# Attention of two inputs on one core: unread products counted per slot, VectorE's exponentials paced apart and eight a unit, the last units normalised piecewise

## The chip, the core and the metric

One core of a Trainium2 chip. The metric is the device time of one execution in microseconds (us); the median of several runs is quoted, and the spread. Five engines run side by side: TensorE (PE in the profile, its weight loads PEld), VectorE (DVE), ScalarE (ACT), GpSimd (POOL) and SyncE (SP), which issues most transfers.

## The reference

Two attention blocks with 32 heads of 16 columns, on 2048 tokens of 512 columns each, bf16. Block A attends to everything, block B to the last 256 positions. Cut to what matters:

```python
qkv = (x @ wqkv).reshape(B, S, 3, H, Dh)          # S=2048, H=32, Dh=16
scores = einsum("bhqd,bhkd->bhqk", q, k) * Dh ** -0.5
# B alone: positions outside 0 <= i - j < 256 get -1e9
o = einsum("bhqk,bhkd->bhqd", softmax(scores), v).reshape(B, S, D) @ wo
return concatenate([a, b], axis=-1)
```

## The kernel before

Block A alone has 2048 x 2048 x 32 exponentials. Work is cut into *units* (four heads by 512 queries), units into *tiles* (128 keys by 512 queries of one head), and three tiles make a *slot*: three score products on TensorE into a score buffer of three PSUM banks (two such buffers), one exponential of 1536 columns on ScalarE. The values of earlier slots are multiplied into one accumulator bank. Everything else shares one spare bank ("ms"): projections, guard rows, and tiles whose exponential VectorE computes by a bit trick (a copy for each tile, and three passes for each two). The order is fixed in advance by a small pacing model: `PITCH` is a slot, `queued` tells it what VectorE has to do, `by` asks whether that will be done in time.

Some words that come back: a *window slot* is a slot of block B. *Padded keys* are those of the first two groups of heads, projected straight into the layout that the scores need. A *guard row* is an extra row of the queries, made from their absolute values and the largest keys, that takes a bound off the scores before the exponential. An *unread product* is a matmul whose result nobody uses. In the lines of the traces `sps` are the score buffers, `ms` is the spare bank, `op` the accumulator, `pT` what ScalarE's exponentials write, `dy` VectorE's copies of scores and `pD` its own exponentials.

```python
PACE_D = (2, 2, 2, 1)      # groups of four tiles a unit for VectorE, from the ninth unit on
...
def scores(self, slot):    # for the slot after next
    ...
    if b == 0 and self.filled < 2 and jb.inst == 0:
        self.work += 0.22   # a product that nobody reads, to keep TensorE's clock up
        self.nc.tensor.matmul(sps[:, 0, 0:WARM], lhsT=kT[...], rhs=qT[...], start=True, stop=True)
    ... # the real scores then overwrite it
...
def slots(self):
    ...
    groups[-1:-1] = poly    # values of VectorE's tiles: all ahead of the unit's last group
...
def q_evac(...):            # projection of queries; guard() two slots later
        gs = self.tile([8, 512], BF16, "gs", 1)          # one buffer
        self.nc.vector.tensor_copy(out=gs[:], in_=b[0:8, :])
        self.nc.sync.dma_start(qd[:, DH, :], gs[:])
...
def end(self, i, p, g):     # the last two units of block A
    rec = self.tile([P, 512], FP32, "oc", 2)
    nc.vector.reciprocal(out=rec[:], in_=op[:])           # straight from the accumulator
    ... copy op to osb, then for both halves: ones x rec on TensorE, multiply on VectorE
...
def run(self):
    for s, sl in enumerate(slots):
        self.exps(sl); ...; self.scores(slots[s + 2]); self.values(); ...
        # one list of tasks, VectorE's tiles among them (they count double)
        credit = min(credit + min(rate, 2.5), 3.0)
        ...
        while credit >= 1.0 and self.fill(s, tasks, done):
            credit -= 1.0; self.filled += 1; self.work += 0.4
        if self.work < 0.8 and self.open is None and self.by(self.freed, 0.9):
            self.busy(2 if self.work < 0.6 else 1)        # unread products into the spare bank
```

Of the kernel before, what the change touches and what calls it, by code (L numbers as in the profile page):

```python
# [14 lines left out]
P = 128  # L15
H = 32
DH = 16
# [25 lines left out]
PACE_D = (2, 2, 2, 1)  # L43
XRING = 5
FIRST_B = 6
WARM = 512
# [56 lines left out]

class _Kernel:

    def __init__(self, ctx, tc, tensors, out):
        self.tc, self.nc = tc, tc.nc
        self.t = tensors
        self.out = out
        pool = lambda name, **kw: ctx.enter_context(tc.tile_pool(name=name, **kw))  # L110
        self.consts = pool("consts", bufs=1)
        self.sb = pool("sb", bufs=1)
        self.ps = pool("ps", bufs=1, space=bass.MemoryType.PSUM)
        self.dram = pool("dram", bufs=1, space=bass.MemoryType.DRAM)
        self.xT, self.w, self.wo, self.kT, self.v, self.qT = {}, {}, {}, {}, {}, {}
        self.acol, self.negas, self.oT = {}, {}, {}
        self.op, self.od = {}, {}
        self.later = []
        self.slot = self.ended = self.closed = -1
        self.pend, self.guards, self.dq = [], [], []  # L120
        self.open = self.mid = None
        self.filled = 2
        self.vec = self.freed = self.op_free = 0.0
        self.last_poly = -1
# [17 lines left out]
    def busy(self, n):  # L142

        b = self.bank()
        for _ in range(n):
            self.nc.tensor.matmul(b[:], lhsT=self.ident[:], rhs=self.junk, start=True,  # L146
                                  stop=True)
# [35 lines left out]
    def more_constants(self):  # L183
# [26 lines left out]
        top = self.tile([8, 512], BF16, "gs", 1)  # L210
        nc.gpsimd.memset(top[:], TOP)
        for t in self.qd:
            nc.gpsimd.dma_start(t[:, DH + 1, :], top[:])
# [145 lines left out]
    def q_evac(self, i, p, pr, bank, copy):  # L359
        qs = self.tile([P, 512], BF16, "qs", 2)  # L360
        mq = self.tile([P, 512], BF16, "mq", 2)
# [9 lines left out]
        def guard():  # L371
            b = self.bank()
            self.nc.tensor.matmul(b[0:8, :], lhsT=w[:], rhs=mq[:], start=True, stop=True)
            gs = self.tile([8, 512], BF16, "gs", 1)
            self.queued(OP, True)
            self.nc.vector.tensor_copy(out=gs[:], in_=b[0:8, :])  # L376
            self.nc.sync.dma_start(qd[:, DH, :], gs[:])
# [36 lines left out]
    def last_out(self, i, p):  # L414
# [12 lines left out]

        def first():
            for qc in range(4):
                for c in range(NC):  # L430
                    mm(qc, c)

        def finish():
            obs = self.tile([P, SLOT, 512], BF16, "pT", 6)
            for qc in range(4):
                mm(qc, NC)
                ob = obs[:, qc, :] if qc < SLOT else self.tile([P, D], BF16, "ob", 2)[:]
                (nc.scalar.copy if qc % 2 else nc.vector.tensor_copy)(out=ob, in_=banks[qc])
                q0 = p * 512 + qc * P
                (nc.scalar if qc % 2 else nc.sync).dma_start(  # L440
                    self.out[q0:q0 + P, i * D:(i + 1) * D], ob)
# [12 lines left out]
    def pad_k_evac(self, gg, c, bank):  # L454
# [4 lines left out]
        else:  # L459
# [3 lines left out]
                                     op=ALU.max, apply_absolute_value=True)  # L463

    def pad_q_evac(self, gg, bank):
        nc = self.nc
        if gg == 0:
# [3 lines left out]
        mq = self.tile([P, 512], BF16, "mq", 2)  # L471
        nc.vector.tensor_scalar(out=mq[:].bitcast(U16), in0=qT.bitcast(U16),
                                scalar1=0x7FFF, scalar2=None, op0=ALU.bitwise_and)
        return mq

    def pad_guard(self, gg, mq):
# [8 lines left out]
        qT = self.padq[:, gg, :]  # L485
        nc.vector.scalar_tensor_tensor(out=qT, in0=qT, scalar=self.top[:], in1=b[:],
# [29 lines left out]
    def scores(self, slot):  # L516
        sps = self.ps.tile([P, SLOT, 512], FP32, name="sps", tag="sps", bufs=2)
        for b, jb in enumerate(slot["jobs"]):
# [4 lines left out]
            if b == 0 and self.filled < 2 and jb.inst == 0:  # L523

                self.work += 0.22
                kT, k0 = self.kT[jb.inst, jb.g // 2, jb.subs[0][0] // 4]
                self.nc.tensor.matmul(sps[:, 0, 0:WARM], lhsT=kT[:, gg, k0:k0 + P],  # L527
                                      rhs=qT[:, gg, 0:WARM], start=True, stop=True)
# [40 lines left out]
    def poly_steps(self, group):  # L569
# [3 lines left out]
        p, g, kt = group[0].p, group[0].g, group[0].subs[0][0]  # L573

        def step(jb):
# [3 lines left out]
            if half == 0:  # L579
# [4 lines left out]
            kT, k0 = self.kT[0, g // 2, kt // 4]  # L584
            k0 += (kt % 4) * P
            nc.tensor.matmul(b[:], lhsT=kT[r, g % 2, k0:k0 + P],  # L586
                             rhs=self.qT[0, p, g // 2][r, g % 2, :], start=True, stop=True,
                             tile_position=(32 * jb.j, 0))
# [29 lines left out]
    def values(self):  # L618


        while self.pend:
            group, last = self.pend[0]
            if any(jb.ready is None or jb.ready > self.slot for jb in group):
                return
            key = group[0].key
# [5 lines left out]
            op = self.op[key]  # L631
            self.pend.pop(0)
            self.work += 0.33
            for jb in group:
                h = 4 * jb.g + jb.j
                for kt, q0, q1, o in jb.subs:
                    self.nc.tensor.matmul(op[32 * jb.j:32 * jb.j + 32, q0:q1],  # L637
                                          lhsT=self.v[jb.inst, kt][:, h * VP:h * VP + 32],
                                          rhs=jb.pT[:, o:o + q1 - q0],
                                          start=(jb.j not in self.started), stop=False,  # L640
                                          tile_position=(0, 32 * jb.j), skip_group_check=True)
                    self.started.add(jb.j)
            if last:
                self.epilogue(*key)
                self.ended = self.slot

    def load_ends(self):

        self.wend = self.tile([P, 2, D], BF16, "kTb", KRING_B)
# [7 lines left out]
    def end(self, i, p, g):  # L657


        nc = self.nc  # L660
        op = self.op[i, p, g]
        ones = self.tile([P, 32], FP32, "den", 2)
        nc.gpsimd.memset(ones[:], 1.0)
        rec = self.tile([P, 512], FP32, "oc", 2)
        nc.vector.reciprocal(out=rec[:], in_=op[:])
        osb = self.tile([P, 512], FP32, "osb", 2)
        (nc.scalar.copy if self.mid else nc.vector.tensor_copy)(out=osb[:], in_=op[:])
        if self.mid:
            self.mid()
        o = self.tile([P, 512], BF16, "oTa", 5)  # L670
        b = self.bank()
        for q in (slice(0, 256), slice(256, 512)):
            for j in range(GH):
                r = slice(32 * j, 32 * j + 1)
                nc.tensor.matmul(b[32 * j:32 * j + 32, q], lhsT=ones[r, :], rhs=rec[r, q],
                                 start=True, stop=True, tile_position=(32 * j, 32 * j))
            nc.vector.tensor_mul(out=o[:, q], in0=osb[:, q], in1=b[:, q])
        self.closed = self.slot
        self.queued(5.0, True)
        self.op_free = self.vec  # L680
        self.oT.setdefault((i, p), []).append(o)

    def epilogue(self, i, p, g):
# [4 lines left out]
        if (i, p) == (0, NPASS - 1) and g >= NG - 2:  # L688
            self.end(i, p, g)
# [40 lines left out]
    def start(self):  # L730
# [71 lines left out]
        nv = 4  # L802
        for t in range(nv):
            vb = tile_("op", 1) if t % 2 else self.bank()
            self.v_mm(0, t, vb[:], range(NC), (0, HV))
            self.v_evac(0, t, vb[:], nc.scalar.copy, (0, HV))
        self.busy(3)
        self.pad_guard(0, mq)
        self.busy(4)
# [3 lines left out]
    def slots(self):  # L813
# [9 lines left out]
        for u in order:  # L823
            groups = [u[k:k + GH] for k in range(0, len(u), GH)]
            k = ua.index(u) if u[0].inst == 0 else -1
            n = PACE_D[k % len(PACE_D)] if k >= FIRST_D else 0
            poly, groups = groups[:n], groups[n:]
# [4 lines left out]
            groups[-1:-1] = poly  # L832
            pend += [(group, group is groups[-1]) for group in groups]
# [71 lines left out]

    def fill(self, s, tasks, done):
# [8 lines left out]
        t = self.cur  # L915
        t["steps"].pop(0)()
# [5 lines left out]
    def run(self):  # L922
        done = set(self.start())
        self.vec = self.freed = self.op_free = 0.0
        slots, self.pend = self.slots()
        tasks = self.plan(slots, done)
        credit = 0.0
        self.scores(slots[0])
        self.scores(slots[1])
        for s, sl in enumerate(slots):  # L930
# [8 lines left out]
            self.work = 0.33  # L939
# [9 lines left out]
            rate, total = 0.0, 0  # L949
            for t in tasks:  # L950
                if t["nb"] <= s:
                    total += len(t["steps"]) * (2 if t["name"][0] == "d" else 1)
                    rate = max(rate, total / max(1, t["due"] - s))
            credit = min(credit + min(rate, 2.5), 3.0)
            self.filled = 0
# [4 lines left out]
            while credit >= 1.0 and self.fill(s, tasks, done):  # L960
                credit -= 1.0
                self.filled += 1
                self.work += 0.4
            if self.work < 0.8 and self.open is None and self.by(self.freed, 0.9):
                self.closed = s
                self.busy(2 if self.work < 0.6 else 1)
        while self.pend:
            self.slot += 1
            self.values()
        assert not tasks and not self.guards, [t["name"] for t in tasks]  # L970
# [52 lines left out]
```

## Time and profile before

| | |
|---|---|
| time, median of 4 runs | 1098.9 us (1088.8 to 1101.4) |
| busy: ScalarE / TensorE / VectorE | 94% / 89% / 58% |
| mean clock of TensorE in the profiled run | 0.970 |
| exponentials on ScalarE | 771, 727 of them of 1536 columns |

The prediction below shows the lines that carry the reading. Two more stretches matter. The first is TensorE's timeline just before one of the half-clock stretches (start, length, engine, line, operation, result and operands, shape, count, and in brackets the idle time before it):

```profile
820.13 0.38 PE L527 MATMUL sps<-qTa,kTa 128*128 128x512 bf16 x1 [0.63 <-ACT pT L559]
820.44 0.39 PE L532 MATMUL sps<-qTa,kTa 32*128 32x512 bf16 x3
820.76 0.40 PE L637 MATMUL op<-pT,va 128*32 128x512 bf16 x4
821.48 0.38 PE L527 MATMUL sps<-qTa,kTa 128*128 128x512 bf16 x1 [0.31 <-ACT pT L559]
821.79 0.39 PE L532 MATMUL sps<-qTa,kTa 32*128 32x512 bf16 x3
822.11 0.40 PE L637 MATMUL op<-pT,va 128*32 128x512 bf16 x4
822.82 0.59 PE L527 MATMUL sps<-qTa,kTa 128*128 128x512 bf16 x1 [0.31 <-ACT pT L559]
```

These are thin slots: one unread product, three scores, four values, and then idle time. The last line is the same product as the first, but takes 0.59 us instead of 0.38: the clock has been halved in between, although TensorE stood still for no longer than 0.63 us at a time. It stayed halved for 20.5 us.

The second is the start. The guard of the first keys could be subtracted at 20.29, and the first exponential came 2.2 us later:

```profile
20.29 0.75 DVE L486 SCALAR_TENSOR_TENSOR qTa<-qTa,top,ms 128x512 bf16<-128x512 bf16 x1 [1.80 <-PE ms L484]
...
21.09 1.02 PE L146 MATMUL ms<-ident 128*128 128x512 bf16 x4 [0.84 <-DVE qTa L486]
...
22.05 0.60 PE L532 MATMUL sps<-qTa,kTa 32*128 32x512 bf16 x6
22.48 2.79 ACT L559 ACTIVATE pT<-sps 128x1536 bf16<-128x1536 f32 x2 [2.99 <-PE sps L532]
```

Four unread products wait for the spare bank and stand ahead of the first scores.

### The profile page before, as it was taken

The page shows a single profiled execution, that of the slowest core. Times are in us where ns is not written, and L with a number is a line of the kernel's source. Part 1 is how long each engine was busy: PE and PEld are TensorE (multiplying, and loading weights), DVE is VectorE, ACT ScalarE, POOL GpSimd, SP SyncE. Part 2 cuts the span into 40 slices and gives each one's busy share as a digit, 9 for nine tenths or more (in the row PEclk, how much of TensorE's full clock was granted, in tenths as well). Part 3 has the DMA queues.
Part 4 walks back from the last instruction along what each step waited for, and adds up shares of the span by engine and source line. Part 5 has one row for each costly group of instructions (what it writes and reads, how often), then busy time and mean ns, then how long its engine had stood idle before and what let it go on. Part 6 is the DMA issues. An engine that isn't in the chain of part 4 may idle for free.

```text
span 1097.5 us, 18628 instructions
## 1 busy us (share of the span) xinstructions
PE 973.1 (89%) x7583; PEld 322.0 (29%) x7661; DVE 636.7 (58%) x844; ACT 1031.8 (94%) x788; POOL 20.3 (2%) x101
## 2 busy tenths in 40 slices
PE   7899888889988899988998889998899999989877
PEld 4333222233323233222332233323232332322212
DVE  3342231126868578883687755777574776576733
ACT  5899999999999999999999899999998999999976
POOL 6000000000000000000000000000000000000000
PEclk9999999999999999999999899999996999997989
DMA  7021531222412123121130411212101221010101
GB/s 231 1 83 35 135 112 35 63 66 74 117 59 76 44 84 94 59 85 41 51 112 20 123 41 42 81 60 89 45 30 59 76 74 60 31 50 20 58 3 39
DMA packets 72358, 73.04 MB, mean 67 GB/s; under 512 B 22584, under 2 KB 55888, under 8 KB 72272
## 3 DMA queue, kind: packets, MB, share of 16 engines
q1 hardware_dynamic: 69072, 67.88, 20.4%
q10 hardware_dynamic: 2432, 1.84, 0.5%
q0 software_dynamic: 768, 2.13, 0.5%
q8 instruction: 60, 0.98, 0.4%
q14 instruction: 26, 0.21, 0.1%
HBM read 38.65 MB, written 31.07 MB: 64 GB/s over the span
## 4 chain that ended last, share of the span: by engine, by line
ACT 50%; PE 29%; issue 11%; DVE 8%; DMA 1%; SPq 0%; ACTq 0%; DVEq 0%
ACT pT L559 50%; PE sps L532 6%; PE op L637 6%; PE ms L242 6%; PE sps L527 4%; PE sps L541 4%; DVE dy L589 2%; PE ms L586 2%; PE ms L146 1%; DMA kTa<-in_A_x_dram 1%; DVE dh L600 1%; DVE pD L610 1%; DVE gs L376 0%; DVE qs L362 0%; DVE ob L407 0%
## 5 line engine op out<-in xcount | busy, mean ns | idle before, releaser
L559 ACT ACTIVATE pT<-sps 128x1536 bf16<-128x1536 f32 (+2 forms) x771 | 1020.8, 1484 | 46.0 <-PE sps L532 29.7
L527 PE MATMUL sps<-qTa,kTa 128*128 128x512 bf16 x580 | 227.4, 392 | 70.6 <-ACT pT L559 62.6
L532 PE MATMUL sps<-qTa,kTa 32*128 32x512 bf16 x1880 | 259.7, 397 | 1.5 <-ACT pT L559 1.3
L637 PE MATMUL op<-pT,va 128*32 128x512 bf16 x1880 | 193.4, 402 | 0.3 <-DVE osb L695 0.2
L589 DVE COPY dy<-ms 128x512 f32<-128x512 f32 x168 | 115.4, 687 | 132.8 <-PE ms L586 131.3
L532 PEld LDWEIGHTS <-kTa 32*128 32x128 bf16 x1880 | 62.9, 91 | 289.5 <-issue 289.1
L600 DVE SCALAR_TENSOR_TENSOR dh<-dy 128x1024 f32<-128x1024 uint16 x84 | 102.4, 1219 | 1.6
L610 DVE SCALAR_TENSOR_TENSOR pD<-dh,dy 128x1024 uint16<-128x1024 f32 x84 | 102.2, 1217 | 1.1
L604 DVE SCALAR_TENSOR_TENSOR dh<-dy,dh 128x1024 f32<-128x1024 uint16 x84 | 102.0, 1215 | 0.9
L527 PEld LDWEIGHTS <-kTa 128*128 128x128 bf16 x580 | 56.4, 97 | 130.3 <-issue 108.2
L637 PEld LDWEIGHTS <-va 128*32 128x32 bf16 x2048 | 51.2, 94 | 111.2 <-issue 108.6
L541 PE MATMUL sps<-mask,ident 128*128 128x128 bf16 (+1 forms) x640 | 78.7, 249 | 0.0
L586 PE MATMUL ms<-qTa,kTa 32*128 32x512 bf16 x168 | 65.5, 390 | 5.8 <-DVE kst L260 1.2
L695 DVE COPY osb<-op 128x512 f32<-128x512 f32 x62 | 42.7, 689 | 35.1 <-PE op L637 34.9
L532 PE MATMUL sps<-qTb,kTb 32*128 32x384 bf16 (+2 forms) x704 | 59.8, 276 | 3.4 <-ACT pT L559 1.7
L146 PE MATMUL ms<-ident 128*128 128x512 bf16 x172 | 53.7, 382 | 9.7 <-DVE dy L589 2.2
L260 DVE CAST kst<-ms 128x512 bf16<-128x512 f32 x28 | 19.3, 690 | 60.2 <-PE ms L242 60.2
L541 PEld LDWEIGHTS <-ident 128*128 128x128 bf16 x640 | 43.7, 98 | 32.7 <-issue 30.0
L362 DVE TENSOR_SCALAR qs<-ms 128x512 bf16<-128x512 f32 x31 | 21.2, 685 | 48.2 <-PE ms L242 48.0
L407 DVE CAST ob<-ms 128x512 bf16<-128x512 f32 x28 | 19.3, 690 | 47.0 <-PE ms L242 46.8
L242 PE MATMUL ms<-wv,xT 128*128 128x368 bf16 (+2 forms) x171 | 37.4, 315 | 2.9 <-DVE padmax L462 0.8
L637 PE MATMUL op<-pT,vb 128*32 128x384 bf16 (+2 forms) x704 | 38.0, 281 | 0.1
(102 smaller groups left out, 445.1 us busy)
## 6 DMA issues: line engine op xcount, KB each, us to landing
od<-osb SPq DMA_DIRECT2D x62, 256.0 KB
oc<-od SPq DMA_DIRECT2D x31, 256.0 KB
rb<-rd SPq DMA_DIRECT2D x31, 256.0 KB
kTb<-kd SPq DMA_DIRECT2D x16, 256.0 KB
qTb<-qd SPq DMA_DIRECT2D x16, 256.0 KB
qd<-qs SPq DMA_DIRECT2D x31, 128.0 KB
qTa<-qd SPq DMA_DIRECT2D x15, 256.0 KB
kd<-kst SPq DMA_DIRECT2D x28, 128.0 KB
```

The source lines that it names most:

```text
L146: self.nc.tensor.matmul(b[:], lhsT=self.ident[:], rhs=self.junk, start=True, stop=True)
L242: self.nc.tensor.matmul(bank, lhsT=lhs(c), rhs=rhs(c), start=(c == 0), stop=(c == NC - 1))
L527: self.nc.tensor.matmul(sps[:, 0, 0:WARM], lhsT=kT[:, gg, k0:k0 + P], rhs=qT[:, gg, 0:WARM], start=True, stop=True)
L532: self.nc.tensor.matmul(sps[:, b, o:o + q1 - q0], lhsT=kT[r, gg, k0:k0 + P], rhs=qT[r, gg, q0:q1], start=(o == jb.subs[0][3]), stop=not jb ...
L541: self.nc.tensor.matmul(sps[:, b, o:o + P * len(kind)], lhsT=self.ident[:], rhs=m, start=False, stop=True, skip_group_check=True)
L559: nc.scalar.activation(out=pT[:, b:e, :n], in_=sps[:, b:e, :n], func=ACT.Exp, scale=LN2 / 128, bias=-127 * LN2)
L586: nc.tensor.matmul(b[:], lhsT=kT[r, g % 2, k0:k0 + P], rhs=self.qT[0, p, g // 2][r, g % 2, :], start=True, stop=True, tile_position=(32 * ...
L589: nc.vector.tensor_copy(out=y[:, half, :], in_=b[:])
L600: nc.vector.scalar_tensor_tensor(out=st["h"][:], in0=low, scalar=-65536.0, in1=low, op0=ALU.add, op1=ALU.mult)
L604: nc.vector.scalar_tensor_tensor(out=st["h"][:], in0=low, scalar=65536.0 * POLY[1], in1=st["h"][:], op0=ALU.add, op1=ALU.mult)
L610: nc.vector.scalar_tensor_tensor(out=out.bitcast(U16), in0=st["h"][:], scalar=POLY[0] * 2.0 ** -41, in1=flat, op0=ALU.mult, op1=ALU.add)
L637: self.nc.tensor.matmul(op[32 * jb.j:32 * jb.j + 32, q0:q1], lhsT=self.v[jb.inst, kt][:, h * VP:h * VP + 32], rhs=jb.pT[:, o:o + q1 - q0], ...
```

## The change

Its intent: hold TensorE's clock with as few unread products as will do, keep them out of the slots that have no room, give VectorE its tiles in its own rhythm and one seventh more of them, and shorten the start and the end. The core of the diff (cuts marked):

```diff
-PACE_D = (2, 2, 2, 1)
+PACE_D = 2
...
     def scores(self, slot):
-            if b == 0 and self.filled < 2 and jb.inst == 0:
-                self.work += 0.22
-                ... one product of keys and queries
+            if b == 0 and jb.inst == 0:
+                self.busy(sps[:, 0, :], 2 - self.whole)
...
     def q_evac(...)                       # mq becomes a ring of three
-            gs = self.tile([8, 512], BF16, "gs", 1)
-            self.nc.vector.tensor_copy(out=gs[:], in_=b[0:8, :])
+            self.nc.vector.tensor_copy(out=mq[0:8, :], in_=b[0:8, :])
...
     def pad_k_evac(...)
+        self.queued(2 * OP + 0.05, True)
...
     def values(self):
+            late = self.poly_pend.get(key, [])
+            if key in self.op and late and self.done_by(late[0]):
+                self.value(key, late.pop(0))      # VectorE's tiles as they come
+                continue
...
     def end(...)
+        nc.vector.tensor_copy(out=osb[:, q0:q1], in_=op[:, q0:q1])
+        def invert(q):
+            nc.vector.reciprocal(out=rec[:, q:q + 128], in_=osb[:, q:q + 128])
+            ...                                  # the spread comes a slot later
+        self.dq += [lambda q=q: invert(q) for q in range(q0, q1, 128)]
...
     def slots(self):
+            if u is ua[-1]:
+                (groups, ends), n = _parts(groups), 1   # last unit: queries 0-255, then 256-511
...
     def fill(...)
+        self.whole += 1 if t["name"][0] in "dv" else 2
...
     def run(self):
+        polys = [t for t in tasks if t["name"][0] == "d"]
+        tasks = [t for t in tasks if t["name"][0] != "d"]
...
+            if poly_credit >= 1.0 and self.open is None and self.fill(s, polys, done):
+                poly_credit -= 1.0
+            must = self.open is not None
+            while (credit >= 1.0 or must) and self.fill(s, tasks, done):
                 credit -= 1.0
-            if self.work < 0.8 and self.open is None and self.by(self.freed, 0.9):
-                self.closed = s
-                self.busy(2 if self.work < 0.6 else 1)
+                must = False
...
     # start(): the first value projections go to score banks, the guard is issued after the third
     # last_out(): two of the four last output blocks are stored before the end
```

## The prediction

> **What bounds the kernel now.** I read the page's busy shares and 40 slices first, then the groups, then ScalarE's and VectorE's timelines at the three places where ScalarE stood idle longest.
>
> ```profile
> PE 973.1 (89%) x7583; PEld 322.0 (29%) x7661; DVE 636.7 (58%) x844; ACT 1031.8 (94%) x788; POOL 20.3 (2%) x101
> ...
> ACT  5899999999999999999999899999998999999976
> ...
> PEclk9999999999999999999999899999996999997989
> ```
>
> ScalarE is busy 94% of the span, and nine or more tenths of nearly every slice, so it bounds the kernel. The TensorE clock dips in three or four slices, and those are slices where ScalarE dips too.
>
> ```profile
> L559 ACT ACTIVATE pT<-sps 128x1536 bf16<-128x1536 f32 (+2 forms) x771 | 1020.8, 1484 | 46.0 <-PE sps L532 29.7
> L527 PE MATMUL sps<-qTa,kTa 128*128 128x512 bf16 x580 | 227.4, 392 | 70.6 <-ACT pT L559 62.6
> L146 PE MATMUL ms<-ident 128*128 128x512 bf16 x172 | 53.7, 382 | 9.7 <-DVE dy L589 2.2
> ```
>
> 771 exponentials are the work. Their own idle time ends with the scores of TensorE (L532), so every lost microsecond is TensorE being late. L527 and L146 are products nobody reads: 752 of them, seven before the first exponential, there to keep the clock up.
>
> The chain that ended last gives the pitch of undisturbed exponentials: starts at 99.81, 101.14 and 102.47, so 1.33 us for 1536 columns (busy spans overlap a little, hence 1484 ns each).
>
> ```profile
> 99.81 1.24 ACT pT L559
> 101.14 1.24 ACT pT L559
> 102.47 1.25 ACT pT L559
> ```
>
> 727 exponentials of 1536 columns x 1.33 = 966.9 us. The other 44 (1152 to 256 columns) at the smallest start-to-start time of each form (1.01 to 0.26 us) are 27.5. **Floor of the loop: 994.4 us.** The first exponential starts at 22.48, the last at 1085.13, so it ends at 1086.46. The loop took 1064.0, and 69 us of it are lateness; before it 22.5, after it 11.0.
>
> I sorted the lateness (start to start, less the floor of the form) by what TensorE did just before:
> - half clock: 15.9 us, in six stretches of 3.4 to 20.5 us (65 us together; one of 6.8 is at the start and costs 1.6)
> - the reciprocal of the last unit but one: 5.84 us
> - one bank eviction that waited for a transfer: 2.81 us
> - TensorE at work for more than 1.33 us in a slot, at full clock: 28.8 us in 113 pieces
> - TensorE waiting for VectorE to empty the one spare bank: 13.9 us (scores copies 5.2, padded keys 3.8, guards 2.4, rest 2.5)
> - pieces under 0.05 us: 2.
>
> The second and third, in the timelines (start, length, then in brackets the idle time before and what ended it):
>
> ```profile
> 1053.52 3.36 DVE L665 RECIPROCAL oc<-op 128x512 f32<-128x512 f32 x1
> ...
> 1060.45 4.18 ACT L559 ACTIVATE pT<-sps 128x1536 bf16<-128x1536 f32 x3 [5.44 <-PE sps L532]
> ```
>
> ```profile
> 621.45 0.68 DVE L376 CAST gs<-ms 8x512 bf16<-8x512 f32 x1 [1.91 <-DMA qd<-gs]
> ```
>
> **What the Trainium skill says.** "TensorE: Matmul & The Clock Gate", Part 1, "What's actually happening": the clock is either half or full, and activity in a free-running 3.4 us window decides. The trace agrees: only 0.5 and 1.0 occur, stretches are multiples of 3.41, and one begins within each of the two long stalls above. Three others begin after three to four slots with only one unread product, scores and values, so such slots are too thin. The same page, "Wait — 56ns, not 53.3ns?", has 215.7 ns between 512-column products; two unread ones here stand 0.216 apart. "ScalarE: Activation LUTs", "What ACT_TABLE_LOAD costs", gives 186 ns + 0.833 ns a column less about 93 of overlap, 1.37 us for 1536 columns; the trace has 1.33, which I use. No page gives a VectorE reciprocal's time; here 512 columns take 3.36 us, five times a copy (0.69).
>
> **The change, part by part.** I counted instructions in both builds and priced each run of matmuls with the spacing the trace shows at full clock: one unread product 0.31, a second +0.216, three scores 0.32, four values 0.33, each further four +0.216, one VectorE tile's score 0.32, two projection products 0.44, masks 0.43 to 0.60.
>
> 1. *Eight tiles a unit on VectorE*: 188 tiles instead of 168 (23 units x 8 + 4). ScalarE loses 20 x 512 columns: 720 full exponentials and 44 others, 957.6 + 27.9 = 985.5 us. **Saves 8.9.** VectorE gains 20 x (0.69 + 3 x 1.22 / 2) = 50 us, to about 690 of the span, still beside ScalarE. Between 400 and 500 it was already 81% busy, so there it gets tight.
> 2. *Unread products counted*: 681 instead of 752. Each slot of the full attention is filled up to two, placed in its own score bank ahead of the scores, so they wait neither for VectorE nor for the spare bank; slots with projections get none. A slot of two unread products, scores and values costs 0.53 + 0.32 + 0.33 = 1.18, under 1.33. Half-clock lateness: I keep 4 of 15.9 (1.6 at the start, the rest one more stretch). Saves 12.
> 3. *Values of VectorE's tiles as they come*, no burst of 12 at a unit's end; unread products never in window slots; an opened bank closed in the next slot. Sums per slot: window slots fall from 1.40 to 1.27 us on average, the others stay at 1.18. If a slot may be 0.32 late before ScalarE notices, the excess over 1.33 adds to 29.5 before (the trace has 28.8, so that slack is right) and to 14.6 after. Saves 14.
> 4. *Guard rows written into a ring of three* instead of one buffer: the 2.81 goes. Padded keys now declared to the pacing (2 x 0.69 + 0.05), so the spare bank isn't asked for too early: of 13.9 I keep 8. Saves 9 together.
> 5. *Last unit but one*: the result is copied first (0.69), inverted in four pieces of 128 columns (3.36 / 4 = 0.84 each), spread later. Nothing waits. I keep 0.5 of 5.84. Saves 5.3.
> 6. *Start*: value projections go to score banks and the guard is issued after the third. It could start when its weights are ready (VectorE L481 ends at 18.48; it started at 19.87), and four unread products no longer stand between guard and scores behind a wait (1.0 us). First exponential at about 20.5: saves 2.
> 7. *End*: the last unit's first 256 queries are normalised before the end, and the last reciprocal is 256 columns, 1.7 us instead of 3.36, two of four output blocks are stored early. But 18 output products (18 x 0.216 = 3.9) then stand on the path, so only about 1.5 of 11.0 goes: 9.5.
>
> Sum: 20.5 + 985.5 + lateness (4 + 0.5 + 0 + 14.6 + 8 + 2 = 29) + 9.5 = **about 1045 us**.
>
> **Rivals.**
> - *VectorE becomes the bound.* For: 81% busy in a stretch, one spare bank, a seventh more tiles; the three-step evaluations (1.22 each) delay copies, and TensorE then waits for the bank in program order. Against: the pacing model only issues when it thinks the bank free, and mean load stays near 66%. If so, bank waits stay at 14 or grow to 25: 1051 to 1062.
> - *The clock still drops.* For: window slots get no unread products, and the rule counts products, not the quantity the gate looks at. Against: every thin slot now has more work than the ones after which it dropped. If half-clock lateness stays at 16, 1057; more, as two unread products at half clock make a slot 2.1 us.
> - *Unread products ahead of the scores delay them.* They sit between the release of a bank and its scores: 0.53 + 0.32 = 0.85 of 1.33, slack 0.4. A projection or VectorE score in front uses this up. That would leave item 3 at nothing: 1059.
> - *Gain only as large as ScalarE's lost columns* (all lateness reappears elsewhere): 1097 - 9 - 5 = 1083.
>
> **Range and chances.** Each of the first three rivals alone leaves 1051 to 1062, two together about 1070; better than expected (no half clock after the start, bank waits at 5) is 1036. Range 1033 to 1066. The time before spreads from 1088.8 to 1100.3, mostly by how many half-clock stretches a run has. Faster by over 2% means under about 1075.6: 0.94; within 2%: 0.05; slower: 0.01.
>
> **What would show each step.** 764 exponentials with 720 full ones, still 1.33 apart; ScalarE busy near 1022. Half-clock stretches after the first 50 us: none or one. No ScalarE idle over 2 us inside the loop. VectorE near 690 busy. The idle time before the exponentials falls from 46 to about 20. First exponential near 20.5, last one ended 9.5 before the end. Wrong if waits of TensorE for VectorE's score copies grow beyond 10 us, if the clock row shows several dips again, or if exponentials come more than 0.1 late in most slots with two unread products.

## The result

The changed kernel took **1049.3 us** (median of 4 runs, 1049.0 to 1056.4), against 1098.9 before. The ratio is 0.9587 (95% interval 0.9529 to 0.9646). A ratio here is the mean time of one kernel's fast runs over that of the other's of the same rounds, so it isn't quite the ratio of the medians.

The page of the profile after, the lines that answer to those of before:

```profile
PE 926.9 (88%) x7638; PEld 318.3 (30%) x7726; DVE 685.7 (65%) x900; ACT 1014.1 (97%) x782; POOL 20.0 (2%) x100
...
ACT  5899999999999999999999999999999999999996
...
PEclk9999999999999999999999999999999999999998
...
L574 ACT ACTIVATE pT<-sps 128x1536 bf16<-128x1536 f32 (+3 forms) x764 | 1002.9, 1486 | 15.2 <-PE sps L547 7.7
L155 PE MATMUL sps<-ident 128*128 128x512 bf16 x681 | 221.8, 380 | 69.1 <-ACT pT L574 58.2
```

ScalarE is busy 97% of the span, the dips of the clock row are gone, seven exponentials fewer are issued, and the idle time ahead of them fell from 46.0 to 15.2 us. VectorE carries 49 us more and is still only 65% busy.

The places of before, in the timelines of after: the start, the last unit but one, and the last reciprocal.

```profile
18.52 0.39 PE L501 MATMUL ms<-mq,padneg 128*128 128x512 bf16 x1
...
20.18 5.69 ACT L574 ACTIVATE pT<-sps 128x1536 bf16<-128x1536 f32 x4 [0.70 <-PE sps L547]
```

```profile
1021.85 0.64 PE L700 MATMUL ms<-oc,padneg 1*32 1x256 f32 x8 [0.53 <-DVE oTa L703]
...
1023.25 4.33 ACT L574 ACTIVATE pT<-sps 128x1536 bf16<-128x1536 f32 x3 [0.93 <-PE sps L547]
...
1028.12 0.95 DVE L716 RECIPROCAL oc<-osb 128x128 f32<-128x128 f32 x1
...
1038.08 1.76 DVE L706 RECIPROCAL oc<-op 128x256 f32<-128x256 f32 x1 [1.71 <-PE op L665]
```

The first exponential starts at 20.18 instead of 22.48. The last unit but one makes ScalarE idle for 0.93 us instead of 5.44. What is left there comes from the spread of its two halves through the one spare bank (0.53 of TensorE waiting for VectorE's product).

Among the waits (who waited, for whom, us in total, times, longest), one of the expected savings is missing:

```profile
PE ms L251 <- DVE padmax L476: 3.5, 4, 1.1
PE ms L251 <- DVE dy L605: 2.3, 7, 0.7
```

To compare kernels I split each span in four: the start of the first exponential, the *floor* (each exponential at the smallest start-to-start time of its size, 1.33 us for 1536 columns), the *lateness* (what start-to-start times add to it), and the end after the last one. The four add up to the span. The lateness is then sorted by what TensorE did just before the late exponential, by a program of mine. Where TensorE stood still for VectorE for less than about 0.2 us, the program counts the piece as work beyond the pitch and not as a wait.

| profiled run | span | first | floor | lateness (of it around half clock) | end | clock |
|---|---|---|---|---|---|---|
| before | 1097.5 | 22.5 | 994.4 | 69.2 (15.9) | 11.5 | 0.970 |
| after | 1047.6 | 20.2 | 985.5 | 31.8 (0.7) | 10.1 | 0.997 |

Of the 50 us, 37 are lateness, 9 floor, 2.3 start and 1.4 end. The kernel before was profiled in one of its runs with a low clock: in the 21 runs of it that stand beside the experiments the mean clock is 0.965 to 0.985, with 0.979 in the middle. So, by these clocks, the 15.9 us around half clock are more than most of its runs have.

### The profile page after: what moved, and what is told of

It is laid out like the page before. It is cut to its first block, busy times and chain, and to the rows that moved or that the text cites. A ratio compares the mean times of both kernels' runs of the same rounds, so it can differ in the third digit from the quotient of the medians.

```text
span 1047.6 us, 18755 instructions
## 1 busy us (share of the span) xinstructions
PE 926.9 (88%) x7638; PEld 318.3 (30%) x7726; DVE 685.7 (65%) x900; ACT 1014.1 (97%) x782; POOL 20.0 (2%) x100
## 3 DMA queue, kind: packets, MB, share of 16 engines
q1 hardware_dynamic: 69216, 68.01, 21.4%
## 4 chain that ended last, share of the span: by engine, by line
ACT 61%; PE 21%; issue 11%; DVE 5%; DMA 1%; ACTq 0%; DVEq 0%
ACT pT L574 61%; PE sps L547 5%; PE op L665 4%; PE ms L251 4%; PE sps L155 3%; PE sps L556 2%; PE ms L602 1%; DMA kTa<-in_A_x_dram 1%; DVE dy L605 1%; DVE dh L616 1%; DVE dh L620 1%; DVE osb L733 1%; PE sps L433 0%; DVE pD L626 0%; DVE kTa L474 0%
## 5 line engine op out<-in xcount | busy, mean ns | idle before, releaser
L574 ACT ACTIVATE pT<-sps 128x1536 bf16<-128x1536 f32 (+3 forms) x764 | 1002.9, 1486 | 15.2 <-PE sps L547 7.7
L155 PE MATMUL sps<-ident 128*128 128x512 bf16 x681 | 221.8, 380 | 69.1 <-ACT pT L574 58.2
L547 PE MATMUL sps<-qTa,kTa 32*128 32x512 bf16 (+1 forms) x1920 | 249.4, 378 | 10.6 <-ACT pT L574 2.5
L605 DVE COPY dy<-ms 128x512 f32<-128x512 f32 x188 | 129.1, 687 | 93.0 <-PE ms L602 91.3
L665 PE MATMUL op<-pT,va 128*32 128x512 bf16 (+1 forms) x1920 | 186.8, 383 | 1.5 <-ACT pT L574 0.9
L155 PEld LDWEIGHTS <-ident 128*128 128x128 bf16 x681 | 63.7, 96 | 170.3 <-issue 157.5
L620 DVE SCALAR_TENSOR_TENSOR dh<-dy,dh 128x1024 f32<-128x1024 uint16 x94 | 114.4, 1217 | 1.4
L602 PE MATMUL ms<-qTa,kTa 32*128 32x512 bf16 (+1 forms) x192 | 71.6, 376 | 9.4 <-DVE kst L269 2.0
L556 PEld LDWEIGHTS <-ident 128*128 128x128 bf16 x640 | 43.6, 97 | 32.0 <-issue 29.2
L371 DVE TENSOR_SCALAR qs<-ms 128x512 bf16<-128x512 f32 x31 | 21.4, 689 | 40.3 <-PE ms L251 39.5
L547 PEld LDWEIGHTS <-kTb 32*128 32x128 bf16 x704 | 24.5, 92 | 36.7 <-issue 31.5
L344 DVE CAST va<-ms 128x368 bf16<-128x368 f32 (+1 forms) x28 | 12.4, 442 | 35.6 <-PE ms L251 35.6
```

Source lines behind the costliest of these rows:

```text
L155: self.nc.tensor.matmul(bank, lhsT=self.ident[:], rhs=self.junk, start=True, stop=True)
L547: self.nc.tensor.matmul(sps[:, b, o:o + q1 - q0], lhsT=kT[r, gg, k0:k0 + P], rhs=qT[r, gg, q0:q1], start=(o == jb.subs[0][3]), stop=not jb ...
L556: self.nc.tensor.matmul(sps[:, b, o:o + P * len(kind)], lhsT=self.ident[:], rhs=m, start=False, stop=True, skip_group_check=True)
L574: nc.scalar.activation(out=pT[:, b:e, :n], in_=sps[:, b:e, :n], func=ACT.Exp, scale=LN2 / 128, bias=-127 * LN2)
L602: nc.tensor.matmul(b[:, o:o + q1 - q0], lhsT=kT[r, g % 2, k0:k0 + P], rhs=self.qT[0, p, g // 2][r, g % 2, q0:q1], start=True, stop=True, t ...
L605: nc.vector.tensor_copy(out=y[:, half, :], in_=b[:])
```

## The experiments

Twelve kernels ran, four to a call; those of a call ran on one chip and shared the runs of the kernel before. "Undo" kernels are the changed kernel with one part taken back. All gave correct results. Splits are of the profiled run, as in the table above.

| run | median us (range of 4) | ratio to before | lateness (half clock) | clock |
|---|---|---|---|---|
| *first chip*: again | 1051.7 (1049.4 to 1052.1) | 0.9594 | 34.0 (2.9) | 0.993 |
| u_pace | 1057.9 (1056.8 to 1058.3) | 0.9653 | 31.6 (2.9) | 0.997 |
| u_oldunread | 1060.0 (1055.9 to 1060.5) | 0.9661 | 41.9 (6.4) | 0.988 |
| u_burst | 1054.5 (1052.4 to 1056.2) | 0.9623 | 38.0 (4.2) | 0.990 |
| *second chip*: u_nounread | 1116.6 (1114.5 to 1126.5) | 1.0210 | 97.2 (83.6) | 0.764 |
| u_one | 1114.2 (1104.6 to 1124.2) | 1.0141 | (profile in the slow state) | |
| b_unread | 1085.8 (1083.8 to 1087.7) | 0.9911 | 54.0 (5.6) | 0.991 |
| u_shared_open | 1070.0 (1066.9 to 1072.3) | 0.9765 | 44.9 (3.7) | 0.992 |
| *third chip*: u_end | 1062.5 (1058.1 to 1062.8) | 0.9680 | 40.6 (4.2) | 0.991 |
| u_gs | 1053.5 (1051.6 to 1058.1) | 0.9604 | 32.8 (2.0) | 0.994 |
| u_alt | 1061.5 (1058.6 to 1062.7) | 0.9666 | 44.2 (18.3) | 0.971 |
| f_both | 1047.7 (1046.7 to 1048.4) | 0.9544 | 29.4 (0.8) | 0.998 |

The kernel before had medians of 1094.4, 1095.3 and 1096.8 in the three calls.

### The yardstick

The changed kernel, not edited.

> The changed kernel once more, as the yardstick for the runs beside it. Theory: 1049 us when no half-clock stretch falls into the loop, 1056 when one does (one of its four runs so far was 1056.4 at a mean clock of 0.986). Lateness of the exponentials 32 us in the profiled run.

1051.7 us. In this profile a half-clock stretch of 6.8 us falls into the loop and costs 2 us. So one or two us between runs of these kernels are such stretches, and differences under 2 us are not read below. Some runs have more of them: one of the changed kernel's first four took 1056.4 us at a mean clock of 0.986.

### Eight tiles a unit

```diff
-PACE_D = 2
+PACE_D = (2, 2, 2, 1)
-            n = PACE_D if k >= FIRST_D else 0
+            n = PACE_D[k % len(PACE_D)] if k >= FIRST_D else 0
```

> Undoes one part: VectorE takes seven tiles a unit on average again (2, 2, 2, 1 groups), all else as changed. Theory (ScalarE's own work is the bound): 20 tiles x 512 columns more, 727 full exponentials, +8.9 us of floor at unchanged lateness (32 +- 3): 1058. Rival (VectorE is near its limit, and fewer tiles shorten TensorE's waits for it): lateness falls by the same amount and the time stays within 3 us of 1049.

6.1 us more than the yardstick. ScalarE's full exponentials, by form:

```profile
L574 ACT ACTIVATE pT<-sps 128x1536 bf16<-128x1536 f32 x727 | 982.9, 1538 | 14.8 <-PE sps L547 9.2 <-PE sps L556 4.3
```

727 of them again and a floor of 994.4, 8.9 higher, with the lateness where it was (31.6 against 31.8 and 34.0). The theory holds: the tiles are worth what they take from ScalarE, and VectorE's larger load costs little (2.4 us of lateness at most, by the yardstick's profile). Versions with twelve tiles in some units did not build, because results were asked for before the plan had made them; so with this planner the lever is at its end.

### Unread products: the old rule

```diff
-                self.busy(sps[:, 0, :], 2 - self.whole)
+                if self.whole < 0:                     # before the first two slots, as changed
+                    self.busy(sps[:, 0, :], 2 - self.whole)
+                elif self.filled < 2:
+                    self.work += 0.22
+                    self.busy(sps[:, 0, :], 1)
...
+            if self.work < 0.8 and self.open is None and self.by(self.freed, 0.9):
+                self.closed = s
+                self.busy(self.bank()[:], 2 if self.work < 0.6 else 1)
```

> Undoes one part: the unread products by the old rule (one ahead of the scores when fewer than two fills, one or two at the slot's end into the spare bank when the slot looks light, in window slots too); 764 of them instead of 681. Theory: two losses come back: window slots rise from 1.27 to 1.37 us of TensorE work and the summed excess over the pitch by 11 us, and half-clock stretches cost 5 to 15 us more: 1063 to 1075, lateness 45 to 58. Rival A (the clock doesn't depend on the rule, only the window slots do): 1060 at a mean clock of 0.997. Rival B (the rule doesn't matter, the other parts made the gain): within 4 us of 1049.

8.2 us more than the yardstick, less than the theory said and near rival A, but with more half-clock stretches than that allows (of the 7.9 us of lateness that its profile has beyond the yardstick's, 3.5 lie there). The larger part is crowding: TensorE at work beyond the pitch at full clock rose from 17.5 to 21.5 us, and its waits for VectorE's score copies from 1.5 to 3.1. With 2 us of half clock from run to run, the two parts are not settled more closely than that.

### The same rule alone, in the kernel before

```diff
-            if b == 0 and self.filled < 2 and jb.inst == 0:
-                ...
+            if b == 0 and jb.inst == 0:
+                for _ in range(2 - self.whole):
+                    self.nc.tensor.matmul(sps[:, 0, :], lhsT=self.ident[:], rhs=self.junk,
+                                          start=True, stop=True)
...
-            if self.work < 0.8 and self.open is None and self.by(self.freed, 0.9):
-                self.closed = s
-                self.busy(2 if self.work < 0.6 else 1)
```

> The kernel before with one part of the change alone: unread products counted per slot up to two, in the score bank, none in window slots. Theory: half-clock lateness falls from about 16 to about 7 (the stalls of 5.8 us at the last unit but one and of the late guard row still trip the gate), the excess sums fall by 8 us from the window slots: 1098 - 17 = 1081, lateness 53. Rival (the rule matters only together with the new pacing): within 5 us of the kernel before.

The lateness came out as expected, 54.0 for 53, and that around half clock at 5.6. In time it is 9.5 us under the kernel before of the same chip (1095.3, itself faster than the 1098.9 that the expectation started from), little more than half of the 17 expected. The stalls that the rule does not touch stay: 6.7 us at the last unit but one.

### How many unread products it takes

None in the loop (11 are left at the start by the trace, not the 7 of the text below):

```diff
-                self.busy(sps[:, 0, :], 2 - self.whole)
+                self.busy(sps[:, 0, :], 2 - self.whole if self.whole < 0 else 0)
```

> The changed kernel without unread products in the loop (7 stay, before the first two slots). Theory (they pay for themselves by holding the clock): most of the full-attention slots run at half clock, mean clock below 0.8; at half clock a slot with a projection costs 0.53 + 0.55 + 0.9 = 2.0 us and a window slot about 2.3, so the time grows by 50 to 200 us: 1100 to 1250. Rival (the other work keeps the clock up by itself): TensorE has 0.2 us less a slot, lateness falls by 5 to 8 us, 1042 to 1046.

A ratio of 1.021 against 0.959: it is slower than the kernel before. The clock row and the exponentials of its page:

```profile
PEclk9999675676578866787678997788776788666658
...
L574 ACT ACTIVATE pT<-sps 128x1536 bf16<-128x1536 f32 (+3 forms) x764 | 1014.4, 1454 | 69.2 <-PE sps L547 37.5
```

From the fifth slice on the clock is half for much of the time, and the idle time before the exponentials goes from 15.2 to 69.2 us. 84 of the 97 us of lateness lie around half clock. So the products that nobody reads earn their 222 us of TensorE time.

One:

```diff
+                self.busy(sps[:, 0, :], (2 if self.whole < 0 else 1) - self.whole)
```

> The changed kernel with each slot filled up to one product instead of two (about 230 unread instead of 681). Theory: the thin slots are then like those of the kernel before or thinner, so half-clock stretches come back with 10 to 40 us of lateness: 1060 to 1090, mean clock 0.85 to 0.96. Rival (one is enough): excess over the pitch falls from 14.6 to 6.9 in the sums, 1041 to 1046 at a mean clock of 0.997.

The theory allowed for 1060 to 1090, and the time is above that. It is nearly as bad as none (1.014 against 1.021, and the intervals, 1.006 to 1.022 and 1.015 to 1.027, overlap). The three fast runs are 1104.6, 1107.7 and 1120.7, at mean clocks of 0.853 to 0.826. The fourth, 1124.2, is classed slow, and the profile fell into it, so I read no split from it.

Two and one in turn:

```diff
+                self.busy(sps[:, 0, :],
+                          (2 if self.whole < 0 else 2 - self.slot % 2) - self.whole)
```

> Slots filled up to two products and to one in turn (about 456 unread instead of 681 or 231). Theory (the gate looks at the share of busy columns over some slots and the mark lies between one and two products a slot): the result lies between, with some half-clock stretches: 1055 to 1095. Rival (only runs of several thin slots trip it, so every second slot is enough): excess sums fall from 14.6 to 9.5, 1045 to 1048 at a clock over 0.98.

1061.5 us, 14 above f_both and 8 above u_gs of the same chip. Its clock row has three dips:

```profile
PEclk9999999999989999996999999999999899999999
```

Every second slot full is not enough, so the rival is refuted. But it brings most of the gain: with 231 unread products the time is 1114, with 456 it is 1061.5, and with all 681 another 8 to 14 us less. So the steep part lies between one a slot and two in every second slot. These runs place it no closer, and they don't tell what quantity the clock follows. TensorE beyond the pitch at full clock fell as the sums said (17.5 to 12.9 us), but 18.3 us around half clock took it back.

### The pacing apart

VectorE's tiles back in the one list, counted double, and an opened bank closed only when there is credit, at seven tiles a unit:

```diff
-        polys = [t for t in tasks if t["name"][0] == "d"]
-        tasks = [t for t in tasks if t["name"][0] != "d"]
+        polys = []
...
-            must = self.open is not None
+            must = False
```

> Undoes the pacing: VectorE's tiles share one list and one credit with the projections again, and an opened bank waits for credit instead of being closed in the next slot. It needs seven tiles a unit on average (with eight the plan does not come out), so it is to be compared with u_pace (1057.9, lateness 32). Theory (the excess sums decide): 22.9 against 13.5, so 9 us more: 1067, lateness 41. Rival (the pacing only makes eight tiles possible and is worth nothing by itself): within 3 us of u_pace.

12 us above u_pace by the ratios (0.9765 and 0.9653, about 1% of 1095), 13.3 by the lateness of the profiles (44.9 and 31.6). The theory said 9. By what TensorE did before late exponentials: work beyond the pitch at full clock 21.4 against 16.0, waits for score copies 4.5 against 2.2, waits for guard copies 2.8 against 0.1. So the separate list and the early closing of the bank, which this run undoes together, are worth at least as much as the 8.9 us of the tiles that they make possible. Which of the two does it was not tested. With eight tiles a unit the shared list ended in a deadlock when it was simulated, so it never ran.

### Values in a burst

```diff
-            if key in self.op and late and self.done_by(late[0]):
-                self.value(key, late.pop(0))
-                continue
+            if (key in self.op and late and end and end[1] == 512 and self.done_by(group)
+                    and all(self.done_by(x) for x in late)):
+                while late:
+                    self.value(key, late.pop(0))
```

> Undoes one part: the values of VectorE's tiles wait for the last group of their unit and come in one burst, as before the change. Theory: the summed excess over the pitch rises by only 2 us (16.8 against 14.6 in the same sums), so 1051, lateness 34. Rival (the bursts were the main part of the 28.8 us that TensorE was late at full clock): +8 or more, 1057 to 1061, with the lateness just after unit ends.

2.8 us, about the theory's size, but the intervals of the two ratios overlap (0.9588 to 0.9658, the yardstick's 0.9561 to 0.9628). The rival's 8 us or more are not reached: the bursts were not the main part of it.

### The last unit but one, inverted in place

```diff
+        if g == NG - 2:
+            nc.vector.reciprocal(out=rec[:], in_=op[:])
+            nc.vector.tensor_copy(out=osb[:], in_=op[:])
+            spread(256)
+            ...
+            return
         nc.vector.tensor_copy(out=osb[:, q0:q1], in_=op[:, q0:q1])
```

> Undoes one part: the last unit but one is inverted in place again, one reciprocal of 512 columns straight from the accumulator, then spread at once, with TensorE waiting behind it. Theory: the stall of 5.8 us returns in place of the 1.2 to 1.6 of the changed kernel, and the half-clock stretch that it sets off costs 1 to 2 more: +5 to +6.5, so 1055 to 1058, lateness 38. Rival (the plan hides it): within 2 us of the yardstick (1051).

More than expected: 1062.5, 9 above u_gs and 15 above f_both of the same chip. VectorE and ScalarE at the place, in their timelines:

```profile
1010.16 3.36 DVE L712 RECIPROCAL oc<-op 128x512 f32<-128x512 f32 x1 [0.60 <-PE op L665]
```

```profile
1017.94 2.96 ACT L574 ACTIVATE pT<-sps 128x1536 bf16<-128x1536 f32 x2 [6.45 <-PE sps L547]
```

The stall is 6.45 us, and within it the clock drops, for 17 us. The profiled run is the fastest of the four (1058.1). The other three are 4.4 us longer, at mean clocks of 0.982 and 0.983 against 0.991: by my estimate from these figures, 38 us at half clock instead of 19. Where those stretches lie was not traced.

### The guard row's buffer

```diff
+            gs = self.tile([8, 512], BF16, "gs", 1)
-            self.nc.vector.tensor_copy(out=mq[0:8, :], in_=b[0:8, :])
-            self.nc.sync.dma_start(qd[:, DH, :], mq[0:8, :])
+            self.nc.vector.tensor_copy(out=gs[:], in_=b[0:8, :])
+            self.nc.sync.dma_start(qd[:, DH, :], gs[:])
```

and the ring of `mq` back to two, which the memory needs.

> Undoes one part: guard rows go through one buffer of 8 rows again instead of the ring of three. Order and sums are those of the changed kernel. Theory: only a guard row whose forerunner's transfer has not landed waits, which in the profile of before happened once (2.8 us with its aftermath): 0 to 3 us, 1050 to 1054. Rival (the buffer doesn't matter, the late transfer was an accident of that run): no wait of VectorE's guard copy for a transfer at all, 1050 to 1052.

The rival held as to the wait; the time, 1053.5, lies 1.5 us above its range, which is not read. In its waits VectorE's guard copy (first line, u_gs) waits for TensorE alone, never for a transfer; in b_unread (second fence), which has the old pacing, the wait for the transfer is there:

```profile
DVE gs L385 <- PE ms L382: 17.2, 23, 1.8
```

```profile
DVE gs L376 <- DMA qd<-gs: 1.5, 1, 1.5
```

Lateness 32.8, as in the changed kernel. The lateness of 2.8 us is gone in the changed kernel, but one buffer would have done under its pacing.

### A version that mends two places

```diff
         self.nc.vector.tensor_reduce(out=self.padmax[:, gg, c:c + 1],
-                                     in_=bank, ...
+                                     in_=kT[:, gg, o:o + 512] if gg else bank, ...
...
         if self.mid:
             nc.vector.reciprocal(out=rec[:, q0:q1], in_=op[:, q0:q1])
-            self.mid()
             nc.scalar.copy(out=osb[:, q0:q1], in_=op[:, q0:q1])
-            spread(128)
+            self.mid((0, 1))               # output blocks 0 and 1, stored
+            spread(128, (2, 3))            # each half spread, then a block's first four products
```

> Two mends on the changed kernel. First: the largest value of the second padded key group is taken from the copy in SBUF instead of from the spare bank, so the bank is free 0.6 us earlier, four times: of 3.6 us of waiting 2.0 to 2.5 should go. Second: at the end ScalarE copies the accumulator before it stores two output blocks, and the spread of the last reciprocals stands ahead of the last eight output products: the end after the last exponential falls from 10.1 to about 8.6. Together 3.5 to 4 us: 1047 against the 1051 of the yardstick. Rival for the first (TensorE waits for the copy itself): under 1 us. Rival for the second (the transfers out set the end): end stays at 10.

1047.7 us, ratio 0.9544 (0.9516 to 0.9571), the lowest of all. It did not run on one chip with the changed kernel, whose ratios are 0.9587 and 0.9594, the intervals overlapping; so a gain of 2 to 5 us is likely, and not settled. By the profile the first mend did what was expected: the lateness of the four exponentials behind padded keys went from 3.6 us to 1.2, and TensorE's wait there from 3.5 to 1.1. (The program above sees only 0.4 of it as a wait: three of the four that are left are 0.19 us long.) The second failed: the end is 9.8 instead of 10.1. The timeline at the end of f_both:

```profile
1035.76 1.76 DVE L710 RECIPROCAL oc<-op 128x256 f32<-128x256 f32 x1 [1.71 <-PE op L666]
...
1037.55 0.37 ACT L711 COPY osb<-op 128x256 f32<-128x256 f32 x1 [2.30 <-DVE oc L710]
1037.82 1.08 ACT L440 CAST pT<-sps 128x512 bf16<-128x512 f32 x2
...
1038.46 0.81 PE L433 MATMUL sps<-wo,oTa 128*128 128x512 bf16 x2
```

ScalarE's copy, which the new order puts first, waits 2.30 us for the reciprocal. The stores of two output blocks stand behind the copy, and by the chain that ended last the next output products (1038.46) wait for the first of these stores. From there on TensorE hardly pauses. So the old path, 3.8 us of output products after the last values, gave way to one that is hardly shorter: the reciprocal, a store, and then the products of two output blocks.

## Why the prediction was right

1045 us was predicted, 1049.3 measured, in the range. Term by term, against the profile after:

- **Floor 985.5**: measured 985.5, with 720 full and 44 other exponentials 1.33 us apart. u_pace shows the 8.9 us of the step by itself.
- **First exponential 20.5**: 20.18. The guard started at 18.52, right behind the weights that were named.
- **Half clock, 4 kept of 15.9**: 0.7 in this run, 2.9 in the yardstick's. The mechanism is shown by u_nounread, u_one and u_alt. Too simple was that the new *rule* does it: with the old rule and all else changed (u_oldunread) lateness around half clock is only 6.4, and with the new rule alone (b_unread) it is 5.6. So either takes most of it away; why the old rule does so well beside the new pacing is not shown.
- **TensorE beyond the pitch, 14.6**: 17.6. The step put three causes into one sum. The runs give them sizes: u_shared_open 12 to 13 in all for the pacing (its waits included, and with seven tiles a unit), u_oldunread 8 for the rule with its clock part, u_burst 3.
- **Bank waits, 8 of 13.9**: 8.3, but for another reason than stated. The reason named was padded keys, and they stayed at 3.6 us (3.8 before); score copies, which the step doesn't name, fell from 5.2 to 1.5. So the size was right by luck. Declaring the time to the pacing model did not move the request by a slot; taking VectorE's second read off the bank did (f_both).
- **Guard rows, 2.8 gone**: gone, but not shown to be due to the ring (u_gs).
- **Last unit but one, 0.5 kept**: 1.2, because both halves of the spread go through one bank. A piece of 128 columns took 0.95 us and not a quarter of 3.36. Undone, it costs 9 us or more, not 5: the stall sets off half clock.
- **Pieces under 0.05 us, 2 kept**: 4.0, what the other terms leave of 31.8.
- **End, 9.5**: 10.1. The end before was 11.5, not 11.0, since the last exponential has 1024 columns and ends earlier than I took it to. The gain of about 1.5 was right (1.4).

The four terms of the prediction add up to 1044.5 and the profiled span is 1047.6. Of the 3.1 us between them lateness is 2.8 (31.8 for 29) and the end 0.6, and the first exponential gives 0.3 back. Within the lateness the errors partly cancel: half clock is 3.3 lower than forecast and the other terms 6 higher in all. That this run met almost no half clock is luck, as the yardstick's 2.9 shows. The time that is measured is 1.7 us above the span.

Of the rivals: VectorE did not become the bound (u_pace). The clock hardly drops, apart from single stretches (one in the yardstick's loop at 151 us, others near the end). Unread products ahead of the scores were not isolated: u_alt has fewer of them and less crowding (12.9 against 17.5 us), so some of that rival may be true, but the clock is worth more. That all lateness reappears elsewhere is refuted by the fall from 69 to 32.

Still open: what exactly the clock gate measures, and where u_end's other runs spend the additional time at half clock.

## What to carry to other kernels

When one engine bounds a kernel at a fixed pitch, split the span into start, floor, lateness and end, and sort the lateness by what the feeding engine did just before; each class then has a remedy and a size that add up. Count filler work that holds a clock per period together with the real work, keep it out of the full periods, and test less of it in more than one step: here a third of it (231 of 681) was worth almost nothing, and two thirds (456) most of the gain. A stall of a few us costs more than its length where it also lets the clock drop.

## What the Trainium skill lacked or had wrong

- "TensorE: Matmul & The Clock Gate", Why this matters for your kernels: the advice is to have no idle gaps over about 3 us. It is not enough here: before three drops of the kernel before no gap was over 0.7 us (those at 659, 823 and 1004 us), and without unread products the mean clock is 0.764 though TensorE is busy seven to nine tenths of every slice. One unread product of 512 columns in a slot of 1.33 us is hardly better than none (fast runs from 1104.6 us; none: from 1114.5), two hold the mean clock at 0.986 to 0.998 in the runs of the changed kernel. Elsewhere the page tells of a kernel whose clock swings because of short pauses between groups of matmuls, but it states no such mark.
- "VectorE: DVE Perf Modes" gives no time for a reciprocal: 512 columns of fp32 take 3.36 us and 256 take 1.76 (read from PSUM), 128 take 0.95 (read from SBUF). For 512 that is five times a copy (0.69).
- "ScalarE: Activation LUTs", What ACT_TABLE_LOAD costs: with 186 + 0.833 N ns and an overlap of about 93, 1536 columns would follow at 1.37 us; here they follow at 1.33, an overlap of 136 ns.
